# An explicit order of 3,392 tasks in place of a list scheduler, in a kernel of attention with memory and a gated feed-forward

## The chip, the cores and the metric

One core of a Trainium2 chip. The metric is the device time of one execution in microseconds (us), as the median of several runs.

## The reference, cut to what matters

`x` has 2,048 rows of 448. The result mixes two branches with a gate for each row:

```python
g = _sigmoid((x * gate_w).sum(-1, keepdims=True))
a = _A_ref(x, A_wq, A_wk, A_wv, A_wo, A_beta)   # 16 heads of 28, 4 segments of 512 rows
b = _B_ref(x, B_w1, B_w2)                       # silu(x @ w1) @ w2, 1792 wide
return g * a + (1 - g) * b
```

Branch A, for each segment s and head: softmax of the scores with a mask inside the segment, times the values; a memory read `phi(q) @ M / (phi(q) @ z)`, where M and z gather `phi(k)^T v` and `phi(k)` of the segments before; the two are mixed by a sigmoid of beta, and `wo` follows.

## The kernel before, in words

**How the work is tiled.** The core keeps 128 partitions. Each float32 operand of a product is split into two float16 halves, a high one and a low one, after a power of two found on the chip has scaled it; a product is then three float16 matmuls (high times high, low times high, high times low) that accumulate in one PSUM bank. `halves` makes the high half (L702 on ScalarE, or L704 on VectorE where both are allowed) and the low half through `rest` (L691 on VectorE as one instruction, or L693 and L694 on GpSimd as two). `product` (L728) issues the matmuls of one such product, cut into tasks of two to five matmuls.

**How it is staged.** First, in `project()`: the inputs are loaded, `scales` finds the powers of two (sums of squares, one small matmul with a matrix of ones at L564, four small VectorE instructions from L568 on), q, k and v are projected for the four segments (`proj`, `vproj`), and the memory is built and read (`memory`, `remember`, `retrieve`). The four value blocks of segment 0 are computed early in float32, before any scale is known (`vearly`, L1091, 16 tasks of two matmul records each). Then, for each of 16 groups of four heads, `maxima` finds the row maxima of the scores (L832 on TensorE, L840 and L845 on VectorE) and `attention` computes the scores again (L1468), their exponentials (L1473, ScalarE), the mask (L1476 and L1479, GpSimd), the halves (L1485 on ScalarE, L1489 on GpSimd) and the product with the values (L1502). The feed-forward runs beside it in two passes over blocks of 128 hidden columns (`unit`: L728 up, L1351 to L1356 with `evict` at L423 on ScalarE or L425 on VectorE, L1373 down). The second pass also applies `wo` to each block of 128 rows (`last_part`, L728 into a bank `sc`), adds it (L1585, L1589) and writes the output. The last row block of all cuts its down products at column 336, so that most of its result can be written before the rest.

**What sets the order.** The code above does not issue instructions; it calls `sch.add` once for each piece of work, with its engine (or a choice of two), a planned length, its inputs, the buffers it takes and a priority. There are 3,392 such tasks, numbered here from 0 in the order in which they are added. `Sched.run` then plays a list scheduler: of the tasks whose inputs are done it picks on each engine the one with the earliest planned start and the best priority, with a table `SHIFTS` of corrections to single priorities, and for a task that may run on two engines `start_of` compares the planned ends with a `SLACK`. What is picked is emitted at once. So each engine's queue is a fixed list in the program, worked off in that order; the semaphores make an instruction wait for its inputs, and everything behind it on its engine then waits too. The planned lengths are in `pe`, `act`, `dve`, `pool`, `few`, `scaled` and the like; at run time they play no part.

**The tasks that are spoken of below**

| tasks | what they are |
|---|---|
| 5, and 6 to 11 | matmuls of zeros: 8 in task 5 (L912), then six tasks of one (L917) |
| 54 to 69 | the early float32 products, four for each of the four row blocks (L1091) |
| 84, 74, 105, 94 | the small matmuls of `scales` for wv, for x of segment 0, for wk, for wq (L564) |
| 75, 85, 95, 106 | the VectorE instructions that follow 74, 84, 94, 105 (L568 to L572) |
| 40, 41 | the load of one quarter of wq, and its sum of squares on ScalarE (L545) |
| 96, 98, 100, 102 | the high halves of wq (96 VectorE, the others ScalarE); 97, 99, 101, 103 the low ones (L691) |
| 77, 79, 81, 83 | the low halves of x of segment 0 (L691); 91 one of wv |
| 124, 165, 166, 167 | first parts of the q products of groups 0 and 1 (L728); the parts after the first need the low halves of wq |
| 233, 234 | squares of the sizes of x of segment 1 (VectorE, L562) and their small matmul (L564); 443, 444 the same for segment 2 |
| 143 | the low half of phi(k) of group 0 (VectorE, L1080), which waits for a ScalarE instruction (L1078) |
| 217, 276 | the low half of q of group 3 (VectorE, L1033), and a k product of segment 1 (L728) that takes the PSUM bank which 217 reads |
| 239, 243, 445 | low halves of x of segment 1 (L691), and the instructions L568 to L572 of segment 2 |
| 968, 971 | low halves of two blocks of w1 |
| 2436, 2444, 2460 | evictions of the first three feed-forward blocks |
| 1006 | the first score matmul of the attention (L1468) |
| 3371 | the last task of the final row block's down product that is 336 columns wide (three matmuls, L1373) |
| 3383 to 3386, 3372 to 3375 | the final row block's `wo` product (11 matmuls), and its down product over the last 112 columns |

Of the kernel before, what the change touches and what calls it, by code (L numbers as in the profile page):

```python
# [50 lines left out]
SLACK = -0.26  # L51
# [5 lines left out]
FULL = 0.111  # L57
# [23 lines left out]
def VP(o, k):  # L81
# [3 lines left out]
PRICE = 191.19  # L85
PRICE2 = 269.85
SLACK2 = -0.48
# [18 lines left out]
SHIFTS = (  # L106
# [45 lines left out]
)  # L152


class Ring:
    def __init__(self, n, make, shared=True):
        self.n, self.make, self.seq, self.shared = n, make, [], shared

    def prev(self):
        k = len(self.seq) - self.n  # L160
# [1503 lines left out]
```

## Time and profile before

| what | us |
|---|---|
| median of three runs | 549.45 |
| lowest and highest of the three | 546.99, 551.03 |
| the profiled execution: its own time | 548.6 |
| the profiled execution: span from first to last instruction | 546.9 |
| TensorE busy, of the span | 536.6 |
| VectorE, ScalarE, GpSimd busy | 436.5, 392.4, 356.8 |

TensorE is busy for 98% of the span, VectorE for 80%, ScalarE for 72%, GpSimd for 65%. A busy TensorE is read with care, since the ends of matmuls are modelled in the trace: consecutive starts in the timeline tell its pace better than the busy time of a row. A view by windows gives, for each stretch of the span, the busy time and the number of instructions of each engine and the granted TensorE clock (`PEclk`, 1.00 is full speed). In a timeline each line is a run of like instructions with its start and its length, and in brackets the idle time of the engine before it and what ended that.

### The profile page before, as it was taken

Reading aid. Unit: us, or ns where it says so; the run is one execution under the profiler, and the core shown is the slowest. Engines: PE = TensorE matmul, PEld = TensorE weight load, DVE = VectorE, ACT = ScalarE, POOL = GpSimd, SP = SyncE. Lnnn points to the kernel's source line nnn. Section 1 sums busy time; section 2 is a strip of 40 time slices with the busy share of each in tenths; the row PEclk is TensorE's granted clock in tenths of the full one; section 3 lists DMA queues with packets and bytes.
Section 4 is the critical chain, followed back from the end, with each engine's and each line's share of the span. In section 5 each row is a group of like instructions: output and inputs, shape, how many; then the busy total and the mean of one; then the engine's idle time right before and its main releaser. Section 6 shows DMA issues by size and latency. Waiting matters only on the chain.

```text
span 546.9 us, 11691 instructions
## 1 busy us (share of the span) xinstructions
PE 536.6 (98%) x4083; PEld 295.3 (54%) x4083; DVE 436.5 (80%) x1065; ACT 392.4 (72%) x660; POOL 356.8 (65%) x542
## 2 busy tenths in 40 slices
PE   9899999999999999999999999999999999999997
PEld 3344555555544456555565555555555555455554
DVE  4889999999879977899765999779998258955553
ACT  5978987866546888888887988879987887501310
POOL 2128997354515778998898988898889997202220
PEclk9899999999999999999999999999999999999999
DMA  8678766535676333422323325555103211769973
GB/s 292 229 220 260 226 183 189 174 97 164 191 200 180 97 111 102 123 86 71 102 75 116 87 72 140 124 151 144 50 20 91 86 50 38 254 155 283 254 201 86
DMA packets 78059, 78.94 MB, mean 144 GB/s; under 512 B 44168, under 2 KB 67720, under 8 KB 78000
## 3 DMA queue, kind: packets, MB, share of 16 engines
q1 hardware_dynamic: 77424, 77.21, 49.1%
q10 hardware_dynamic: 576, 0.99, 0.6%
q8 instruction: 32, 0.52, 0.4%
q14 instruction: 27, 0.22, 0.1%
HBM read 48.41 MB, written 26.09 MB: 136 GB/s over the span
## 4 chain that ended last, share of the span: by engine, by line
PE 83%; DVE 9%; DMA 3%; POOL 2%; issue 1%; ACT 1%; SPq 0%; DVEq 0%; POOLq 0%; ACTq 0%
PE mm L728 22%; PE mm L1373 17%; PE sc L728 10%; PE cc L1373 6%; PE sc L1468 6%; PE cc L1502 6%; PE sc L832 5%; PE cc L728 4%; DVE sc L845 2%; PE sc L1091 2%; DMA rawf<-in_w_dram 1%; PE cc L1145 1%; PE cc L1221 1%; DVE ghl L1356 1%; DVE mm L1353 1%
## 5 line engine op out<-in xcount | busy, mean ns | idle before, releaser
L1489 POOL TENSOR_TENSOR phl<-pf,phl 128x384 f16<-128x384 f32 (+1 forms) x192 | 190.8, 1013 | 27.9 <-ACT phl L1485 27.3
L1473 ACT ACTIVATE pf<-sc,lift,es 128x512 f32<-128x512 f32 (+1 forms) x192 | 126.3, 702 | 26.2 <-PE sc L1468 22.1
L845 DVE CUSTOM_DVE_ANT_0 sc<-sc,mk 128x384 f32<-128x384 f32 (+2 forms) x192 | 105.1, 569 | 22.5 <-PE sc L832 20.7
L1373 PE MATMUL mm<-wb,ghl 128*128 128x448 f16 (+2 forms) x516 | 111.5, 348 | 0.0
L728 PE MATMUL mm<-xh,wa 128*128 128x512 f16 x429 | 108.7, 378 | 0.1
L1373 PEld LDWEIGHTS <-ghl 128*128 128x128 f16 x684 | 64.4, 97 | 53.7 <-issue 0.9
L1485 ACT ACTIVATE phl<-pf 128x1280 f16<-128x1280 f32 x64 | 80.8, 1265 | 9.8 <-POOL pf L1479 9.5
L728 PEld LDWEIGHTS <-wa 128*128 128x128 f16 x572 | 53.7, 97 | 53.4 <-issue 1.5
L1468 PE MATMUL sc<-ring 86*128 86x128 f16 (+3 forms) x256 | 59.9, 299 | 0.5 <-ACT pf L1473 0.3
L832 PE MATMUL sc<-ring 84*128 84x384 f16 (+3 forms) x256 | 57.9, 299 | 1.2 <-DVE mx L840 0.4
L739 POOL TENSOR_TENSOR ol<-ol,ml 128x448 f32<-128x448 f32 x12 | 14.0, 1170 | 53.7 <-DMA ol<-o_scr 36.2
L1502 PEld LDWEIGHTS <-phl 128*128 128x128 f16 x1280 | 41.9, 96 | 9.7
L728 PE MATMUL mm<-xh,wqs 128*128 128x512 f16 x176 | 43.7, 387 | 1.8 <-DVE wqs L704 1.8
L728 PE MATMUL mm<-xh,wks 128*128 128x512 f16 x176 | 43.6, 381 | 0.9 <-DVE stg L1033 0.9
L1479 POOL TENSOR_SCALAR_AFFINE_SELECT pf<-pf 128x384 f32<-128x384 f32 x64 | 33.7, 527 | 15.5 <-ACT pf L1473 15.0
L1502 PE MATMUL cc<-vg,phl 128*128 128x29 f16 (+1 forms) x1280 | 43.6, 182 | 0.0
L745 ACT ACTIVATE oh<-ol,os 128x448 f16<-128x448 f32 x16 | 10.7, 666 | 41.9 <-POOL ol L739 41.2
L1373 PE MATMUL cc<-wb,ghl 128*128 128x448 f16 x168 | 38.3, 352 | 0.0
L1351 ACT ACTIVATE th<-mm,ths 128x512 f32<-128x512 f32 x39 | 26.6, 682 | 15.2 <-PE mm L728 15.2
L728 PE MATMUL cc<-xh,wa 128*128 128x512 f16 x143 | 36.6, 378 | 0.0
L1468 PEld LDWEIGHTS <-ring 86*128 86x128 f16 x256 | 24.2, 97 | 23.0 <-issue 1.1
L728 PE MATMUL sc<-wos,oT 128*128 128x448 f16 x176 | 35.4, 352 | 0.0
(204 smaller groups left out, 923.0 us busy)
## 6 DMA issues: line engine op xcount, KB each, us to landing
rawf<-in_w_dram SPq DMA_DIRECT2D x26, 256.0 KB
rawf<-in_w_dram SPq DMA_DIRECT2D x28, 224.0 KB
v_scr<-vt SPq DMA_DIRECT2D x16, 232.0 KB
vg<-v_scr SPq DMA_DIRECT2D x16, 232.0 KB
xraw<-in_x_dram SPq DMA_DIRECT2D x14, 256.0 KB
q_scr<-stg SPq DMA_DIRECT2D x16, 224.0 KB
ring<-q_scr SPq DMA_DIRECT2D x16, 224.0 KB
k_scr<-stg SPq DMA_DIRECT2D x16, 224.0 KB
```

The lines of the kernel that those rows point to most:

```text
L728: nc.tensor.matmul(ps(), *p[i], start=(i == 0), stop=(i == n - 1))
L739: d = pool(530, lambda: nc.gpsimd.tensor_add(b.v, b.v, m.v), d, e, uses=[b, m], **k)
L832: nc.tensor.matmul(ps.v[:, u:u + n], rg.v[:KS, 0, hh, i * 128:(i + 1) * 128], rg.v[:KS, 1, hh, :n], start=i + t > 0, stop=(i + t > 0 or j ...
L845: nc.vector.tensor_tensor_reduce(r, r, MK[:, L - n:], 1.0, NEG, OP.add, OP.max, mx.v[:, hh, i:i + 1])
L1351: e1 = sact(L, lambda ps=ps, th=th: nc.scalar.activation(th.v, ps.v, AF.Tanh, scale=ths[:, s:s + 1]), m, takes=[th], uses=[ps], prio=p0)
L1373: nc.tensor.matmul(ps.v[:, lo:hi], g.v[:, y, sl], w.v[:, z, lo:hi], start=(j == 0 and i == 0), stop=(j == len(fs) - 1 and i == 2))
L1468: nc.tensor.matmul(ps.v[:, e:e + w], rg.v[:KK, 1, hh, j * 128:(j + 1) * 128], rg.v[:KK, 0, hh, j * 128:], start=True, stop=True)
L1473: ex.append(sact(e + 104, lambda b=b, ps=ps, pf=pf, e=e: nc.scalar.activation(pf.v[:, b, :e], ps.v[:, :e], AF.Exp, bias=lift, scale=es[:, ...
L1479: mk.append(pool(204, lambda pf=pf: nc.gpsimd.affine_select(pf.v[:, :, :128], pf.v[:, :, :128], [[0, 3], [1, 128]], OP.is_ge, 0.0, base=0, ...
L1485: hi = copy(1280, lambda hl=hl, flat=flat: nc.scalar.activation(hl.v[:, 0], flat(), AF.Copy), *mk, takes=[hl], uses=[pf], prio=p0 + 2)
L1489: low = pool(w - u + 22, lambda hl=hl, flat=flat, u=u, w=w: nc.gpsimd.tensor_sub(hl.v[:, 1, u:w], flat()[:, u:w], hl.v[:, 0, u:w]), low, u ...
L1502: nc.tensor.matmul(p[:, i, :2 - z], hl.v[:, z, u:u + 128], vg.v[:, j, hh, :2 - z], start=(z == zs[0] and i == 0), stop=(z == zs[-1] and j ...
```

## The change

The list scheduler is taken out: `offer`, `matmuls`, the candidate lists, the prices and slacks, and the table `SHIFTS`. In their place stands a table `ORDER` that names every one of the 3,392 tasks once, in the order in which it is to be emitted. A negative entry -1-i means task i on the second of its two engines (ScalarE or VectorE: VectorE; VectorE or GpSimd: GpSimd). Seven planned lengths are edited. Against the order that the list scheduler gives, all engines keep their tasks but for 42 that change between two engines: 9 from VectorE to GpSimd (six low halves, 87, 449, 968, 971, 3015 and 3109, and three sums), 1 from GpSimd to VectorE, 19 from VectorE to ScalarE, 13 from ScalarE to VectorE. Within the engines, 465 of TensorE's 1,201 tasks, 206 of ScalarE's and 270 of VectorE's lie outside the longest run of tasks that both orders have in common; TensorE's move by 2.6 places in the mean and by 27 at most.

```diff
-SHIFTS = (
-    (14, 17, 239.16), (41, 41, 29.48), (64, 64, 83.58), (65, 65, -15.52), (95, 95, 613.1), (97, 101, -24633.04),
...
+ORDER = (
+    3, 22, 5, 6, 7, 8, 9, 10, 34, 30, 0, 13, 14, 32, 26, 18, 36, 15, 17, 28, 11, 20, 54, 55, 19, 16, 24, 23, 27, 29, 25, 73,
+    35, 44, 31, 33, 38, 46, 37, 50, 56, 57, 84, 66, 85, 1, 2, 48, 74, 75, 67, -81, 116, 4, 45, 12, 52, 39, -83, 81, 90, 68,
+    42, 40, 47, 58, 78, 847, 91, 163, 59, 79, 69, 70, 51, 49, 53, 43, 41, 83, 187, 122, 21, 60, 61, 156, 76, 105, 94, 106,
+    95, 111, 100, 77, -97, 101, 98, 99, 62, 211, 63, 113, 97, 102, 117, 848, 103, 157, 158, 64, 65, 849, 153, 124, 114, 165,
+    166, 414, 167, 107, 108, 109, 334, 112, 86, 125, 71, 110, 850, 123, 144, 159, 88, 126, 146, 148, 127, 851, 261, 152, 168,
...
+    961, 959, 963, 1006, 2435, 972, 966, 1067, 1066, 2443, 2454, 2455, 2436, 2456, 2457, 1010, 1008, 2444, 2437, 1068, 2450,
+    1005, 973, 967, 2445, 1007, 2462, 1069, 2458, 1011, 2451, 1009, 1020, 974, -2453, 969, 2453, 1156, -969, 2459, 1070,
...
+    3283, 3353, 3333, 3362, 3357, 3363, 3364, 3334, 3335, 3382, 3370, 3379, 3383, 3384, 3385, 3386, 3371, 3372, 3373, 3374,
+    3375, 3330, 3365, 3331, 3366, 3367, 3348, 3387, 3388, 3349, 3389, 3390, 3391,
 )
...
-        while wait is None or wait:
-            best = None
-            for eng, c in self.cand.items():
...
+        while wait if wait is not None else self.at < len(ORDER):
+            i = ORDER[self.at]
+            self.at += 1
+            t = self.tasks[max(i, -1 - i)]
+            t.eng = list(t.costs)[i < 0]
+            s = self.start_of(t, t.eng)
+            assert t.nd == 0 and s is not None, "order"
...
-        return sch.add(("DVE", "POOL"), (0.135 + 0.00104 * cols, 0.3 + 0.0051 * cols), lambda e: fn(eng[e]), deps, port=True, **k)
+        return sch.add(("DVE", "POOL"), (0.135 + 0.00104 * cols, 0.3 + 0.0054 * cols), lambda e: fn(eng[e]), deps, port=True, **k)
...
-                ready = [dve(75, lambda: nc.vector.tensor_mul(v, v, v), *ready, prio=prio)]
+                ready = [dve(250, lambda: nc.vector.tensor_mul(v, v, v), *ready, prio=prio)]
...
-        VREADY[s] = few(1, gate, SCALED[NSEG - 1 - s], SCALED[WV], prio=prio)
+        VREADY[s] = few(0, gate, SCALED[NSEG - 1 - s], SCALED[WV], prio=prio)
...
-        EREADY[s] = few(10, scores, PREADY[s], SCALED[WQ], SCALED[WK], prio=prio + 0.5)
+        EREADY[s] = few(8, scores, PREADY[s], SCALED[WQ], SCALED[WK], prio=prio + 0.5)
```

The three other length edits have the same form (`kscale` 2 to 4, `qscale` 2 to 0.5, `derive` 6 to 7.4).

More of the change, by code (lines that the diff above doesn't have):

```diff
@@ L50 @@
 WIRE = 4.3
-SLACK = -0.26
 LOP = 210.09
@@ L82, in VP @@
     return o + VA + VS * k if o or k > VF else -1.0 + 0.1 * k
-PRICE = 191.19
-PRICE2 = 269.85
-SLACK2 = -0.48
 PVRUNS = [((1, 0), 1)]
@@ L217, in __init__ @@
         self.free = {e: 1.0 for e in self.HOP}
-        self.cand = {e: [] for e in self.HOP}
         self.count = 0
@@ L222, in __init__ @@
         self.wire, self.lands = WIRE, []
-        self.price, self.slack = PRICE, SLACK
-        self.shift = {i: d for a, b, d in SHIFTS for i in range(a, b + 1)}
+        self.tasks, self.at = [], 0
     def add(self, eng, dur, fn, deps=(), takes=(), uses=(), prio=0.0, lat=0.0, port=False, load=None):
         self.count += 1
-        prio += self.shift.get(self.count, 0.0)
         t = Task(eng, dur, fn, [d for d in deps if d is not None], list(takes), list(uses), (prio, self.count), lat, port)
@@ L236, in add @@
                 t.nd += 1
-        if t.nd == 0:
-            self.offer(t)
-        return t
-    def offer(self, t):
-        for e in t.costs:
-            self.cand[e].append(t)
+        self.tasks.append(t)
+        return t
     def ready(self, t, eng):
@@ L265, in start_of @@
                 s = max(s, b.last.end + self.HOP[b.last.eng])
-        if len(t.costs) > 1:
-            o = [e for e in t.costs if e != eng][0]
-            if self.locked(t, eng, s) + t.costs[eng] > self.locked(t, o, max(self.free[o], s)) + t.costs[o] + self.slack:
-                return None
         return self.locked(t, eng, s)
@@ L280, in uncovered @@
         return max(0.0, t.lead - self.tail) if s < self.free["PE"] + 1e-6 else 0.0
-    def matmuls(self, ready):
-        leads = sorted(t.lead for t in ready)
-        def rank(t):
-            nxt = leads[0] if t.lead != leads[0] or len(leads) == 1 else leads[1]
-            if len(leads) == 1 or t.lead == leads[0] and leads[1] != leads[0]:
-                nxt = FULL
-            return t.prio[0] + self.price * (max(0.0, t.lead - self.tail) + max(0.0, nxt - t.tail)), t.prio[1]
-        return min(ready, key=rank)
     def run(self, until=None):
         wait = set(until) if until is not None else None
-        while wait is None or wait:
-            best = None
-            for eng, c in self.cand.items():
-                first = pick = None
-                can = []
-                for t in c:
-                    s = self.start_of(t, eng)
-                    if s is None:
-                        continue
-                    can.append((s, t))
-                    if first is None or s < first - 1e-9 or (s <= first + 1e-9 and t.prio < pick.prio):
-                        first, pick = s, t
-                if eng == "PE" and pick is not None and first < self.free["PE"] + 1e-9:
-                    pick = self.matmuls([t for s, t in can if s <= first + 1e-9])
-                if pick is not None and (best is None or first < best[0]):
-                    best = (first, pick, eng)
-            if best is None:
-                assert wait is None and not any(self.cand.values()), "stuck"
-                return
-            s, t, t.eng = best
-            for e in t.costs:
-                self.cand[e].remove(t)
+        while wait if wait is not None else self.at < len(ORDER):
[5 more added lines that the diff above has]
+            assert t.nd == 0 and s is not None, "order"
             if t.eng == "PE":
@@ L345, in run @@
                 n.nd -= 1
-                if n.nd == 0:
-                    self.offer(n)
             if wait is not None:
@@ L638, in kscale @@
         if s < NSEG - 1:
-            KREADY[s] = few(2, go, SCALED[NSEG - 1 - s], SCALED[WK], *deps, prio=prio)
+            KREADY[s] = few(4, go, SCALED[NSEG - 1 - s], SCALED[WK], *deps, prio=prio)
     def qscale(s, prio):
@@ L646, in go @@
             by(z, z, UP, op0=OP.min)
-        PQREADY[s] = few(2, go, SCALED[NSEG - 1 - s], SCALED[WQ], prio=prio)
+        PQREADY[s] = few(0.5, go, SCALED[NSEG - 1 - s], SCALED[WQ], prio=prio)
     def others(s, prio, bds, own, t_own, t_gh):
@@ L685, in go @@
             by(hso[:, s:s + 1], wide[:, s:s + 1], hs[:, s:s + 1])
-        return few(6, go, SCALED[W1], EREADY[s], GDONE[s], prio=prio)
+        return few(7.4, go, SCALED[W1], EREADY[s], GDONE[s], prio=prio)
     def rest(e, out, a, s, b):
@@ L1320, in infini_mix @@
     BK["cc"].give(BK["mm"])
-    sch.price, sch.slack = PRICE2, SLACK2
     fes = ExitStack()
```

196 rows, old and new, of tables (ORDER, SHIFTS) are left out of this document.

## The prediction

> **What bounds the kernel now.** I read the page first, then its stages by windows, then TensorE's waits and timeline in the stages where it is not full. The page:
>
> ```profile
> span 546.9 us, 11691 instructions
> PE 536.6 (98%) x4083; PEld 295.3 (54%) x4083; DVE 436.5 (80%) x1065; ACT 392.4 (72%) x660; POOL 356.8 (65%) x542
> ```
>
> The windows (per engine: busy us, instructions; then the granted clock):
>
> ```profile
> 0.00:25.00 25.00, 22.14 (x61) 9.38 (x62) 15.77 (x54) 18.07 (x44) 5.86 (x32) 0.94 0.82 278
> 25.00:75.00 50.00, 48.07 (x292) 25.93 (x291) 47.45 (x101) 43.88 (x103) 33.66 (x57) 0.99 0.74 224
> 75.00:160.00 85.00, 84.96 (x548) 47.37 (x547) 77.79 (x173) 57.26 (x120) 45.16 (x87) 1.00 0.56 166
> 160.00:200.00 40.00, 38.53 (x276) 19.98 (x274) 36.77 (x99) 30.81 (x48) 23.04 (x30) 1.00 0.52 143
> 200.00:540.00 340.00, 339.84 (x2890) 190.91 (x2889) 256.46 (x638) 242.42 (x347) 249.05 (x337) 1.00 0.43 118
> 540.00:546.90 6.90, 3.02 (x26) 1.76 (x24) 2.26 (x5) 0.00 (x0) 0.00 (x0) 1.00 0.29 100
> ```
>
> TensorE sets the time everywhere. From 75 to 160 and from 200 to 540 us it is idle for 0.04 + 0.16 us, and a new order can win nothing there. Its idle time is 2.86 us at the start, 1.93 between 25 and 75, 1.47 between 160 and 200, and 3.88 at the end. Every task stays, so TensorE's work stays; an order is worth what it takes from these four numbers, and from the clock.
>
> **The change, part by part.** The code that schedules emits nothing, and the mended lengths emit nothing either: order and engine now come from the table, and the planned start is used in an assertion alone. Their cost is nil and needs no cover. What is left are the places of the tasks, one stage after the other.
>
> *Start.* TensorE's timeline, VectorE's beside it, then two windows:
>
> ```profile
> 4.43 1.37 PE L917 MATMUL mm<-maskb 128*128 128x512 bf16 x4
> 5.63 3.40 PE L1091 MATMUL sc<-raw,xraw 128*128 128x450 f32 x8
> 18.82 1.02 PE L1091 MATMUL sc<-raw,xraw 64*128 64x450 f32 x2
> 19.77 0.60 PE L917 MATMUL mm<-maskb 128*128 128x512 bf16 x2
> 20.21 0.28 PE L564 MATMUL cc<-sums,ones 128*128 128x5 f32 x2
> 22.32 2.74 PE L728 MATMUL mm<-xh,wqs 128*128 128x512 f16 x6 [1.82 <-DVE wqs L704]
> 25.87 3.62 PE L728 MATMUL mm<-xh,wqs 128*128 128x512 f16 x16
> 29.33 4.26 PE L728 MATMUL mm<-xh,wks 128*128 128x512 f16 x19
> ```
> ```profile
> 15.65 0.61 ACT L545 ACTIVATE junk<-raw 128x512 bf16<-128x512 f32 x1
> ```
> ```profile
> 20.54 0.16 DVE L568 TENSOR_REDUCE few<-cc 128x1 f32<-128x5 f32 x1 [0.87 <-PE cc L564]
> 22.84 2.73 DVE L691 SCALAR_TENSOR_TENSOR wqs<-raw,up,wqs 128x512 f16<-128x512 f32 x4
> ```
> ```profile
> 22.30:25.60 3.30, 3.28 (x8) 1.20 (x9) 3.30 (x6) 3.30 (x8) 0.00 (x0) 0.50 0.29 107
> 25.60:27.00 1.40, 1.40 (x8) 0.64 (x7) 1.40 (x3) 1.40 (x4) 0.27 (x1) 1.00 0.36 47
> ```
>
> The last square of wq (task 41) starts on ScalarE at 15.65 and is done before 16.5, but its matmul (94) stands behind all early products and two matmuls of zeros and runs at 20.21. So the scale of wq is late, TensorE idles 1.82 us, and then the clock is granted at 0.50: 8 matmuls in 3.30 us. At full speed 16 take 29.33 - 25.87 = 3.46, so 8 take 1.73, and the slow stretch loses 1.6. Together 3.4 us.
>
> In the table the two matmuls of zeros come before the early products, and 94 before the last four of these (62 to 65). An early product takes 3.40 / 4 = 0.85 us, so 94 runs with 3.4 us of work left behind it. It is not late itself: load 40 and square 41 keep their places on their queues. Ahead of VectorE's part of it (95) stand more pieces than before, and it ends, by my adding up of VectorE's rows, at about 19.2, with the high halves of wq by about 20.7. The early products, behind zeros that now run 0.4 us longer at the front, end between 20.5 and 21.1 (74 now comes after five of them in place of eight and may wait half a microsecond for x's sums). So 124 starts near 21.0, at full clock. Of the gain of 1.3 + 1.6 a part goes at once: the four low halves of wq take 2.73 us on VectorE and end near 23.4, and TensorE, now faster than they, waits some 0.6 us for them. I take 2.3 us. The bounds are 0 (the chain ends where it did) and 3.4 (both losses go).
>
> The Trainium skill (TensorE: Matmul & The Clock Gate, "What's actually happening") says that the clock is halved after an idle window of about 3.4 us, and that these windows run freely. The slow stretch has that length (3.30 us and a rest), but the gap ahead of it was 1.82 us, so here the trace differs: a window that was only half idle was enough. By free windows some executions of before would not have the slow stretch, this step would be worth 0.7 us in them, and the sum would be 2.8.
>
> *25 to 75 us.* TensorE's waits, and VectorE's rows beside the two longest:
>
> ```profile
> PE mm L728 <- DVE stg L1033: 0.9, 1, 0.9
> PE cc L564 <- DVE sums L562: 0.7, 2, 0.4
> ```
> ```profile
> 39.39 0.68 DVE L1080 SCALAR_TENSOR_TENSOR phk<-sc,spk,phk 128x448 f16<-128x448 f32 x1 [1.75 <-ACT phk L1078]
> 39.99 0.15 DVE L562 TENSOR_TENSOR sums<-sums 128x5 f32<-128x5 f32 x1
> 45.95 1.05 DVE L562 TENSOR_TENSOR sums<-sums 128x5 f32<-128x5 f32 x1
> 50.30 1.29 DVE L1033 SCALAR_TENSOR_TENSOR stg<-mm,stg 128x512 f16<-128x512 f32 x2
> ```
> ```profile
> 45.82 1.15 POOL L694 TENSOR_TENSOR xh<-xraw,xh 128x512 f16<-128x512 f32 x1
> ```
>
> Here the queue's head blocks. Task 143 (L1080) waits 1.75 us for ScalarE, with 233 (L562) behind it, for whose matmul TensorE waits. In the table 233 stands five tasks ahead of 143. The 0.9 us are 276's, for the bank that 217 (L1033) reads; 217 goes up nine places, ahead of 239, 445 and 243. These two waits go. The second L562 took 1.05 us in place of 0.15: it ends with GpSimd's L694, at 47.0. It can meet such a piece again. I take 1.3 of the 1.6 us; bounds 0.5 and 1.9.
>
> The Trainium skill (SBUF — State Buffer, on the shared port pair) says that VectorE with two SBUF inputs and a reading GpSimd exclude each other for a whole instruction. The row of 1.05 us agrees. It speaks against the nine pieces moved to GpSimd; what that could cost is the last rival but one.
>
> *160 to 200 us*, waits of TensorE, and the mean durations (third number from the bar) of what moves:
>
> ```profile
> PE sc L832 <- DVE mx L840: 0.4, 1, 0.4
> PE sc L1468 <- ACT pf L1473: 0.3, 1, 0.3
> PE sc L832 <- DVE mx L845: 0.2, 1, 0.2
> ```
> ```profile
> L425 DVE TENSOR_SCALAR ghl<-mm 128x512 f16<-128x512 f32 x23 | 15.8, 686 | 0.5
> L691 DVE SCALAR_TENSOR_TENSOR wa<-rawf,up,wa 128x512 f16<-128x512 f32 x13 | 10.5, 824 | 0.9 <-ACT wa L702 0.9
> L693 POOL TENSOR_SCALAR xraw<-xraw,up 128x512 f32<-128x512 f32 x6 | 9.4, 1572 | 1.0 <-ACT xh L702 1.0
> L694 POOL TENSOR_TENSOR xh<-xraw,xh 128x512 f16<-128x512 f32 x6 | 7.1, 1184 | 0.5
> ```
>
> VectorE is the late one, busy for 36.77 of 40 us. The table takes from it just ahead of this stage 968 and 971 (0.82 us each, to GpSimd, busy 23.04) and evictions 2436, 2444 and 2460 (0.69 each, to ScalarE, busy 30.81): 3.7 us. And the first score matmul (1006) comes five tasks earlier. I take 1.0 of the 1.47 us; bounds 0 and 1.47.
>
> *End.*
>
> ```profile
> 538.48 1.87 PE L1373 MATMUL mm<-wb,ghl 128*128 128x336 f16 x12
> 540.19 2.25 PE L728 MATMUL sc<-wos,oT 128*128 128x448 f16 x11
> 542.47 0.68 DVE L1585 SCALAR_TENSOR_TENSOR ya<-sc,gas,pl 128x448 f32<-128x448 f32 x1 [1.67 <-PE sc L728]
> 543.24 0.81 DVE L1589 SCALAR_TENSOR_TENSOR y<-mm,ogs,ya 128x336 f32<-128x336 f32 x2
> ```
>
> The `wo` product is followed by L1585 and L1589, which set the end. Twelve matmuls of 336 columns take 540.19 - 538.48 = 1.71 us; the table puts three of them (3371) behind that product, under L1585. The product ends 0.43 us earlier, and so does the kernel. Bounds 0 and 0.43.
>
> *Elsewhere* 465 of TensorE's 1,201 tasks stand otherwise in stretches that are full, so they can only lose. If a tenth of 340 us ran like 160 to 200 us, that is 34 x 1.47 / 40 = 1.2. I take half, 0.6; bounds 0 and 3.
>
> Sum: 2.3 + 1.3 + 1.0 + 0.4 - 0.6 = 4.4 us. The profiled execution took 548.6 us, span and 1.7 around it, so it would take 544.2. It lay 0.85 under the median shown, 549.45; on that, I forecast 545.0, 0.8% less. About 1%, or 5.5 us, is what a measurement of this kernel can tell from no change.
>
> **Rivals.**
>
> *All waits go* and nothing new comes: 3.4 + 1.6 + 1.47 + 0.43 + 0.2 elsewhere = 7.1, so 542.3. For it speaks that each wait above has a task that moved; against it that the low halves of wq still follow one another on VectorE.
>
> *The start stays late.* 95 stands behind more VectorE pieces than 94's new place suggests (81, 91, 79, 83, 106). If 106 and 95 end after 20 us, the gap and the slow clock stay, and only 2.1 us are won: 547.3.
>
> *GpSimd's pieces hold VectorE back; slower.* 968 and 971 on GpSimd take 1.57 + 1.18 = 2.75 us each, 5.5 together, where VectorE took 1.65. If VectorE waits them out, as L562 did at 45.95, or the first feed-forward products that need these halves do, TensorE is short of 5.5 us of work just where scores begin. A gap beyond 1.82 us also brings the slow clock, 1.6 more. It decides from about 4.4 us of such idle time; in full it is 7.1 lost against 4.4 won: 552.2. Against it: GpSimd is idle for 17 of 40 us there.
>
> *The order doesn't matter:* semaphores already leave TensorE little idle time and new waits of the same size replace the old: 549.5.
>
> **How the numbers follow.** The forecast 0.54 (its terms give 543 to 547), all waits go 0.18, the start stays late 0.16, GpSimd slower 0.06, no change 0.06. Faster by over 1% is below 543.95: most of the second case and a third of the first, 0.34. Slower by over 1% (above 554.9) is the worse half of the slower rival, 0.03; the rest, 0.63, is within 1%. The range from 541.5 to 549.0 leaves out the two last cases and little at the low end.
>
> **What would show it.** Right: L564 for wq near 17.7 us with L1091 behind it, the first L728 by 21.3 us, the clock at 1.00 after it, no wait of L564 on L562 near 39 us, L728 not waiting for L1033 near 50, TensorE idle under 0.7 us from 160 to 200, and L1373 at 336 columns behind the last L728. Wrong: a granted clock of 0.50 after the first microseconds, new waits of TensorE between 200 and 540 us, or a span above 546.

## The result, and the profile after

| | before | after |
|---|---|---|
| median, us | 549.31 (4 runs, 546.99 to 551.03) | 541.91 (4 runs, 541.10 to 542.12) |
| profiled execution: own time, span | 548.6, 546.9 | 541.86, 539.7 |

The ratio is 0.9865, with a 95% interval from 0.9827 to 0.9903: the table makes the kernel 1.35% faster, 7.4 us (5.3 to 9.5). The forecast was 545.0 in a range from 541.5 to 549.0.

First the head of the page after:

```profile
span 539.7 us, 11686 instructions
PE 533.7 (99%) x4083; PEld 295.1 (55%) x4083; DVE 429.9 (80%) x1051; ACT 396.0 (73%) x666; POOL 376.3 (70%) x556
```

Then the windows that were shown of before (per engine: busy us and instructions; granted clock ahead of the two DMA columns):

```profile
0.00:25.00 25.00, 23.80 (x71) 9.89 (x72) 16.45 (x55) 17.48 (x45) 6.85 (x31) 1.00 0.71 250
25.00:75.00 50.00, 49.47 (x304) 27.02 (x303) 48.47 (x104) 45.21 (x108) 38.57 (x57) 1.00 0.77 231
75.00:160.00 85.00, 84.41 (x549) 47.38 (x548) 78.30 (x174) 59.97 (x123) 46.98 (x94) 1.00 0.63 185
160.00:200.00 40.00, 39.96 (x306) 21.78 (x305) 36.12 (x102) 33.25 (x51) 31.69 (x40) 1.00 0.42 120
```

TensorE is idle for 0.53 us between 25 and 75 us where it was 1.93, and for 0.04 between 160 and 200 where it was 1.47; the clock is 1.00 in all four rows. One idle stretch is new, 0.59 us between 75 and 160. The list of TensorE's waits after has three rows left beside one at the start that both kernels have (a line's number is 72 higher than before, further down 71: L904 was L832, L1147 was L1075, L1422 was L1351):

```profile
PE sc L904 <- ACT th L1422: 0.6, 1, 0.6
PE sc L1147 <- DVE ph L1130: 0.5, 1, 0.5
PE sc L1163 <- DMA raw<-in_wv_dram: 0.2, 1, 0.2
```

TensorE's timeline at the start:

```profile
17.53 0.61 PE L636 MATMUL cc<-sums,ones 128*128 128x5 f32 x4
18.00 3.46 PE L1163 MATMUL sc<-raw,xraw 128*128 128x450 f32 x8
21.39 5.01 PE L800 MATMUL mm<-xh,wqs 128*128 128x512 f16 x22
26.25 4.05 PE L800 MATMUL mm<-xh,wks 128*128 128x512 f16 x18
```

The small matmuls for wk and wq (105 and 94) are one row at 17.53, four early products follow them, and the first scaled product begins at 21.39 with no gap in front of it and no slow stretch behind it: 22 matmuls in 26.25 - 21.39 = 4.86 us, 0.22 each.

**Where the 7.2 us of the span come from.** Idle time alone doesn't say, so the two timelines are compared at instants at which TensorE has done exactly the same set of tasks in both kernels; there the difference of the two starts is what the new order is ahead. Rows of before, then of after, each the first behind such an instant:

```profile
81.99 1.46 PE L728 MATMUL mm<-xh,wqs 128*128 128x512 f16 x6
...
162.38 1.46 PE L728 MATMUL cc<-xh,wa 128*128 128x512 f16 x6
...
188.00 0.73 PE L1373 MATMUL mm<-wb,ghl 128*128 128x448 f16 x3
...
394.12 0.38 PE L832 MATMUL sc<-ring 84*128 84x512 f16 x1 [0.16 <-DVE mx L845]
```
```profile
58.08 0.73 PE L800 MATMUL sc<-wvs,xh 128*128 128x450 f16 x3
...
77.35 1.46 PE L800 MATMUL mm<-xh,wqs 128*128 128x512 f16 x6
...
158.45 0.38 PE L904 MATMUL sc<-ring 84*128 84x128 f16 x4 [0.57 <-ACT th L1422]
...
181.44 0.38 PE L1539 MATMUL sc<-ring 86*128 86x512 f16 x1
...
387.12 0.38 PE L904 MATMUL sc<-ring 84*128 84x512 f16 x1
```

| same work done at (before) | at (after) | ahead | gained since the line above |
|---|---|---|---|
| 29.33 | 26.89 | 2.4 | 2.4 |
| 63.45 | 58.08 | 5.4 | 2.9 |
| 81.99 | 77.35 | 4.6 | -0.7 |
| 162.38 | 158.45 | 3.9 | -0.7 |
| 188.00 | 181.44 | 6.6 | 2.6 |
| 394.12 | 387.12 | 7.0 | 0.4 |
| span's end, 546.9 | 539.7 | 7.2 | 0.2 |

(26.89 lies inside the row at 26.25, three matmuls of 0.215 us on; 63.45 in a row of seven of before that starts at 62.80.) Three stretches won, two lost 0.7 us each to new waits, and the 340 us in which TensorE was full won 0.4.

The loss at 61 us, in the timeline after, VectorE's, GpSimd's and TensorE's rows:

```profile
60.11 1.65 DVE L1130 SCALAR_TENSOR_TENSOR ph<-pe,pp 112x512 f32<-112x512 f32 x1
...
60.05 1.16 POOL L766 TENSOR_TENSOR xh<-xraw,xh 128x512 f16<-128x512 f32 x1
...
61.91 0.57 PE L1147 MATMUL sc<-ident,ph 112*128 112x112 f32 x4 [0.53 <-DVE ph L1130]
```

VectorE's instruction took 1.65 us; it starts 0.06 us behind a GpSimd piece that ends at 61.21, and TensorE waits for it. (Without that piece beside it the same instruction takes 0.67 us, in experiment 11 and also in 7, whose order is that of after up to there: so this wait comes in some executions of the order and not in others.) And the end, TensorE's rows, then VectorE's:

```profile
532.77 2.25 PE L800 MATMUL sc<-wos,oT 128*128 128x448 f16 x11
534.85 1.18 PE L1444 MATMUL mm<-wb,ghl 128*128 128x336 f16 x15
...
535.05 0.68 DVE L1656 SCALAR_TENSOR_TENSOR ya<-sc,gas,pl 128x448 f32<-128x448 f32 x1 [0.99 <-PE sc L800]
536.07 0.81 DVE L1660 SCALAR_TENSOR_TENSOR y<-mm,ogs,ya 128x336 f32<-128x336 f32 x2 [0.33 <-PE mm L1444]
```

The three wide matmuls (3371) now run behind the `wo` product, in the row of 15. L1656 starts 7.42 us earlier than its counterpart at 542.47; L1660, which then waits 0.33 us for those three matmuls, only 7.17 earlier than at 543.24.

### The profile page after: what moved, and what is told of

Read it like the earlier page. It is cut to its first block, busy times and chain, and to the rows that moved or that the text cites. A ratio compares the mean times of both kernels' runs of the same rounds, so it can differ in the third digit from the quotient of the medians.

```text
span 539.7 us, 11686 instructions
## 1 busy us (share of the span) xinstructions
PE 533.7 (99%) x4083; PEld 295.1 (55%) x4083; DVE 429.9 (80%) x1051; ACT 396.0 (73%) x666; POOL 376.3 (70%) x556
## 4 chain that ended last, share of the span: by engine, by line
PE 94%; DMA 2%; ACT 1%; DVE 1%; issue 0%; SPq 0%; DVEq 0%; ACTq 0%
PE mm L800 30%; PE mm L1444 17%; PE sc L800 10%; PE cc L1444 7%; PE sc L1539 6%; PE sc L904 6%; PE cc L1573 6%; PE cc L800 5%; PE sc L1163 1%; DMA raw<-in_wv_dram 1%; PE cc L1217 1%; PE cc L1293 1%; PE sc L1147 1%; DMA xraw<-in_x_dram 1%; PE mm L1163 1%
## 5 line engine op out<-in xcount | busy, mean ns | idle before, releaser
L1560 POOL TENSOR_TENSOR phl<-pf,phl 128x384 f16<-128x384 f32 (+1 forms) x192 | 190.9, 1015 | 17.1 <-ACT phl L1556 15.9
L1544 ACT ACTIVATE pf<-sc,lift,es 128x512 f32<-128x512 f32 (+1 forms) x192 | 128.3, 705 | 24.0 <-PE sc L1539 21.3
L917 DVE CUSTOM_DVE_ANT_0 sc<-sc,mk 128x256 f32<-128x256 f32 (+2 forms) x192 | 106.0, 568 | 27.0 <-PE sc L904 24.4
L800 PE MATMUL mm<-xh,wa 128*128 128x512 f16 x440 | 111.4, 378 | 0.0
L1444 PE MATMUL mm<-wb,ghl 128*128 128x448 f16 (+2 forms) x486 | 107.2, 347 | 0.0
L1556 ACT ACTIVATE phl<-pf 128x1280 f16<-128x1280 f32 x64 | 80.8, 1266 | 5.7 <-POOL pf L1547 3.1
L1539 PE MATMUL sc<-ring 86*128 86x128 f16 (+3 forms) x256 | 61.0, 299 | 0.0
L904 PE MATMUL sc<-ring 84*128 84x256 f16 (+3 forms) x256 | 60.3, 299 | 0.6 <-ACT th L1422 0.6
L1444 PE MATMUL cc<-wb,ghl 128*128 128x448 f16 x198 | 44.9, 352 | 0.0
L1581 DVE TENSOR_REDUCE oraw<-cc 128x116 f32<-128x232 f32 x64 | 25.1, 393 | 19.7 <-PE cc L1573 19.5
L1550 POOL TENSOR_SCALAR_AFFINE_SELECT pf<-pf 128x384 f32<-128x384 f32 x64 | 34.2, 534 | 7.8 <-ACT pf L1544 6.4
L1422 ACT ACTIVATE th<-mm,ths 128x512 f32<-128x512 f32 x40 | 27.4, 684 | 15.9 <-PE mm L800 13.2
```

The source lines that it names most:

```text
L800: nc.tensor.matmul(ps(), *p[i], start=(i == 0), stop=(i == n - 1))
L904: nc.tensor.matmul(ps.v[:, u:u + n], rg.v[:KS, 0, hh, i * 128:(i + 1) * 128], rg.v[:KS, 1, hh, :n], start=i + t > 0, stop=(i + t > 0 or j ...
L917: nc.vector.tensor_tensor_reduce(r, r, MK[:, L - n:], 1.0, NEG, OP.add, OP.max, mx.v[:, hh, i:i + 1])
L1422: e1 = sact(L, lambda ps=ps, th=th: nc.scalar.activation(th.v, ps.v, AF.Tanh, scale=ths[:, s:s + 1]), m, takes=[th], uses=[ps], prio=p0)
L1444: nc.tensor.matmul(ps.v[:, lo:hi], g.v[:, y, sl], w.v[:, z, lo:hi], start=(j == 0 and i == 0), stop=(j == len(fs) - 1 and i == 2))
L1539: nc.tensor.matmul(ps.v[:, e:e + w], rg.v[:KK, 1, hh, j * 128:(j + 1) * 128], rg.v[:KK, 0, hh, j * 128:], start=True, stop=True)
```

## The experiments

The theory: the semaphores' waits go where the prediction placed them, each by its own move, and the table changes nothing else. The rivals: the table or the lengths do something by themselves; what is won early is given back later; single moves would do as much; engines rather than places matter. All kernels are the code after with another table (4 changes one call besides), so their line numbers are those of after, or one higher in 7 and, from the changed call on, in 4. "Control" is experiment 1, and "ahead of control" compares the profiled executions at equal work, as above. Ratios are to the kernel before, run on the same chip. In the diffs of 1, 2, 5 and 6 the table after stands on the minus side; in 3, 4, 9 and 10 the order of before does.

**1. The old order as a table.**

```diff
 ORDER = (
-    3, 22, 5, 6, 7, 8, 9, 10, 34, 30, 0, 13, 14, 32,
+    30, 3, 0, 22, 12, 18, 5, 32, 34, 36, 17, 24, 16, 1,
...
```

> The list order of before, written out as a table, under the code of after with its mended lengths. If table and lengths emit nothing by themselves, this is the program of before: 549.3 us, ratio 1.000, and a clock of 0.50 for 3.4 us near 22 us in every execution, so a mean clock of 0.997. If the windows of the clock run freely, some executions have no slow stretch (mean clock 0.999 or 1.000) and are some 1.6 us shorter. If the mended lengths matter by themselves, the time lies below 549.

Measured: 548.69 (10 runs) against 548.68 (31 runs), ratio 1.0001 [0.9983, 1.0019]. In both traces TensorE, VectorE, ScalarE and GpSimd run the same instructions in the same order. Table and lengths cost and bring nothing that can be measured. Its profiled execution brought a second finding: span 546.0, clock 1.00 throughout, with the same gap as before:

```profile
22.05 1.78 PE L800 MATMUL mm<-xh,wqs 128*128 128x512 f16 x6 [1.82 <-DVE wqs L776]
```

So the same program with the same 1.82 us of idle time has the slow stretch in one execution and not in another. How often, the mean granted clock of an execution tells: in the profiled execution of before, with its one slow stretch, it is 0.997. It is 0.997 or less in 8 of control's 10 executions and in 57 of the 69 of before that stand beside these experiments, and 0.999 or 1.000 in the rest. The 57 took 549.0 us in the mean, the 12 others 548.7.

Against control's profiled execution the table is ahead by 0.9 us at the start rather than 2.4, by 2.6 at the 77 us instant, and by 6.1 us at the end of TensorE's work. The first six steps of the table above are 0.9, 2.3, -0.5, -0.5, 2.4 and 0.7 against it. So between two executions of one program a step differs by up to 0.65 us, beside the 1.5 of the clock.

**2. Only the start: after's table to about 28 us, then the old order.**

```diff
-    928, 236, 198, 143, 375, 178, 415, 182,
+    928, 236, 198, 118, 115, 104, 155, 160, 177, 178, 143, 958, 182,
...
```

> The table of after up to the first 14 parts of q and k products (all engines, some 28 us), then the order of before. Places theory: the start wins 2.4 us, as the progress of TensorE in the two traces has it, and no more: 546.9 us. Rival, that the start only looks shorter because later work is put off: the gain is given back by 75 us, and the time is 549.

Measured: 547.67 (10 runs), ratio 0.9978 [0.9963, 0.9993]. At equal work it is 1.8 us ahead of control at 37 us and 0.7 behind at 50. The waits of TensorE that took it:

```profile
PE mm L800 <- DVE stg L1105: 1.9, 1, 1.9
PE cc L1217 <- DVE phk L1152: 1.2, 2, 0.8
```

The first is the wait for 217 that was 0.9 us in before. TensorE came earlier, VectorE's queue did not, and the wait took up the difference: the start alone is mostly given back 20 us later. It is worth 0.2%.

**3. One move: 94 ahead of the last two early products (64, 65), of 105 between them and of the zeros, in the old order.**

```diff
-    847, 64, 82, 849, 261, 105, 144, 65, 334, 83, 145, 148, 10, 149, 11, 106, 156, 374, 94, 152,
+    847, 82, 849, 261, 144, 334, 83, 145, 148, 149, 156, 94, 64, 105, 65, 10, 11, 106, 374, 152,
```

> The order of before with one task moved: 94, the small matmul for the scale of wq, ahead of the last two early products and the two matmuls of zeros. Places theory: its VectorE part (95) starts when 106 ends, near 19.6 us in place of 20.5, the first L800 comes near 21.5 in place of 22.3, the gap shrinks to 1.0 us and the clock stays at 1.00: about 2 us won, 547.3. If the whole rearrangement of VectorE is needed, the first L800 stays at 22.3 and nothing is won, 549.3.

Measured: 548.70 (10 runs), ratio 0.9999 [0.9981, 1.0018]. TensorE's row, then VectorE's that explains it:

```profile
21.99 0.49 PE L800 MATMUL mm<-xh,wqs 128*128 128x512 f16 x1 [1.43 <-ACT wks L774]
...
20.85 0.69 DVE L1187 SCALAR_TENSOR_TENSOR vt<-mm,rvf,vt 128x448 f16<-128x448 f32 x1 [0.38 <-ACT gate L1185]
21.45 0.48 DVE L776 TENSOR_SCALAR wqs<-raw,up 128x512 f16<-128x512 f32 x1
```

94 is early, but on VectorE, whose order this edit leaves as it was, task 158 (L1187) stands ahead of the high half of wq (96, L776) and waits for ScalarE. The gap is 1.43 us in place of 1.82, and the slow stretch is there too. Moving the one late task isn't enough; the queues behind it have to be rearranged with it.

**4. The gap filled: the zeros behind 94, the second of them nine matmuls.**

```diff
-    148, 10, 149, 11, 106, 156, 374, 94, 152,
+    148, 149, 106, 156, 374, 94, 10, 11, 152,
...
-            END1.append(pe(half(L), lambda: nc.tensor.matmul(
-                wb.v, maskb, maskb[:, None, :].to_broadcast([128, 4, 128]), start=True, stop=True),
+            many = 9 if _ == MORE - 1 else 1
+            END1.append(pe(half(L), lambda many=many: [nc.tensor.matmul(
+                wb.v, maskb, maskb[:, None, :].to_broadcast([128, 4, 128]), start=True, stop=True) for _ in range(many)],
```

> The order of before, with 94 ahead of the two matmuls of zeros and the second of these made nine, so that 2.2 us of zeros fill the gap ahead of the first L800; one part alone, the clock. Clock theory: no slow stretch, and the 1.6 us that it lost are won, with 0.3 us more for 94: 547.4. Rival, that the slow stretch ran under the low halves of wq (VectorE until 25.6 us): TensorE only waits where it was slow, and less than 0.7 us is won: 548.6.

Measured: 548.09 (10 runs), ratio 0.998 [0.9965, 0.9995].

```profile
19.75 2.32 PE L990 MATMUL mm<-maskb 128*128 128x512 bf16 x10
21.90 0.67 PE L800 MATMUL mm<-xh,wqs 128*128 128x512 f16 x2
```

No gap and no slow stretch, at the price of ten matmuls of zeros: the mean granted clock is 0.999 or 1.000 in all ten executions, where 27 of the 31 of before have 0.997 or less. What remains is 0.6 us in the median (0.3 to 1.9 by the interval). That is the size that the rival named, less than the 1.5 by which control stands ahead of before just behind the stretch. Its reason isn't borne out: control, at full clock, is 1.6 us ahead of before at 28 us and still 1.8 at 480. But at the end of TensorE's work 0.9 are left. How much of the 1.5 lasts to the end of an execution stays open; this only bounds the clock's part of the whole gain.

**5. After's table to about 75 us, then the old order.**

```diff
-    434, 371, 482, 483, 484, 875, 387,
+    434, 371, 875, 876, 454, 297, 457, 458, 305,
...
```

> The table of after for the first 120 TensorE tasks and all that goes with them (some 75 us), then the order of before. Against a control execution at full clock, after is 0.9 us ahead by 30 us and 2.6 ahead by 75. Places theory: that lead is kept, since the rest has the waits of before and no more: 548.7 - 2.6 = 546.1. Rival, seen where only the start was changed: queues filled for one order and emptied by another bring new waits at the seam, and the lead is gone: 548.5.

Measured: 549.41 (10 runs) against 549.10 (15), ratio 1.0015 [0.9996, 1.0034]. At equal work it is 3.9 us ahead of control at 50 us, and still so behind 70; at 89.4 us 0.4 are left, and by 180 it is 1.5 behind. The wait, and the windows around it:

```profile
PE cc L1217 <- DVE amr L1299: 3.2, 1, 3.2
```
```profile
85.87:89.28 3.41, 0.35 (x2) 0.10 (x1) 0.64 (x2) 1.28 (x3) 2.60 (x11) 1.00 0.44 150
89.28:92.69 3.41, 3.25 (x20) 2.45 (x20) 3.41 (x10) 2.30 (x7) 2.08 (x3) 0.50 0.44 135
```

At the seam TensorE finds an instruction of the old order whose VectorE work has not come, waits 3.2 us, and gets the half clock for it. This kernel can't tell what the first 75 us are worth, only that it isn't kept by an order that was made for another arrival.

**6. After's table to about 190 us, then the old order.**

```diff
-    1140, 1135, 2517, 1143, 2541, 1064, 1339, 1124, 1002,
+    1140, 1135, 2517, 1339, 1278, 1064, 1002, 1124, 2551,
...
```

> The same to some 190 us, past the stage where scores begin. Places theory: the lead is 4.6 us there, and after that TensorE has nothing left to win but some 0.3 us and the end: 544.1. If the moves between 200 and 540 us are worth more than the traces show, it stays above 545.

Measured: 541.47 (4 runs), ratio 0.9875 [0.9838, 0.9911], the same as the whole table within the intervals. As far as these (some 2 us to either side) can tell, all of the gain is made in the first 190 us, and the new order of the other 350, the end included, is worth nothing.

**7. After, with 968, 971, 2436, 2444 and 2460 back on VectorE.**

```diff
-    2443, 2454, 2455, 2436, 2456, 2457, 1010, 1008, 2444, 2437,
+    2443, 2454, 2455, -2437, 2456, 2457, 1010, 1008, -2445, 2437,
...
-    2453, 1156, -969, 2459,
+    2453, 1156, 968, 2459,
...
```

> The table of after, with five tasks put back on VectorE: the low halves 968 and 971 and the evictions 2436, 2444, 2460. If VectorE's relief by 3.7 us is what won the 2.3 us from 160 to 200 (prediction), TensorE waits for VectorE there again and the time is 543 to 544. If the order alone did it (scores earlier, score and feed-forward tasks dealt out otherwise), it stays at 541.9.

Measured: 542.80 (6 runs), ratio 0.9901 [0.987, 0.9931]; the median is 0.9 us above after's. At equal work it is 1.5 us ahead of the profiled execution of after at 60 us, 0.9 at 158 and 0.7 behind at 169: 2.2 us go there. Part of that is a wait for a transfer at 157.6, where after waits 0.6 for ScalarE:

```profile
PE sc L905 <- DMA ring<-k_scr: 1.2, 1, 1.2
```

The five engines matter by a microsecond or so, in the direction that the prediction had; the intervals of 7 and of after overlap, so this is likely and not shown. Of the lead at 60 us, 0.7 is the wait at 61, which this execution doesn't have, though nothing was changed up to there: VectorE's instruction started 0.6 us ahead of the GpSimd piece, and took its plain length.

```profile
58.82 0.67 DVE L1131 SCALAR_TENSOR_TENSOR ph<-pe,pp 112x512 f32<-112x512 f32 x1
```

**8. After, with two moves against the two new waits:** 287 (the transposes that wait for L1130) three places back, behind 389, and 1069 (the score matmul that waits at 158) behind 2463. As the edit was made, 1069 also came to stand behind 1071, another score matmul.

```diff
-    345, 300, 287, 900, 877, 257, 389, 390,
+    345, 300, 900, 877, 257, 389, 287, 390,
...
-    2462, 1069, 2458, 1011,
+    2462, 2458, 1011,
...
-    2459, 1070, 1021, 2463, 1071, 1072,
+    2459, 1021, 2463, 1071, 1069, 1070, 1072,
```

> The table of after with two TensorE tasks moved behind one ready product each: 287 (the transposes that wait 0.7 us for VectorE near 61 us) behind 389, and 1069 (the first scores of the second group, which wait 0.7 us near 157) behind 2463. If these waits are TensorE's own to avoid, 1.3 us are won: 540.6. Rival: the later tasks hold up their banks and the wait comes back further on: 541.9.

Measured: 543.64 (4 runs), ratio 0.9907 [0.987, 0.9944]: 1.7 us above after in the median. The wait at 61 is gone, but:

```profile
162.54 0.32 PE L904 MATMUL sc<-ring 84*128 84x384 f16 x1 [1.64 <-DVE mx L917]
```

**9. The two moves of the prediction's second step alone:** in the old order, 233 ahead of 143, and 217 ahead of 239.

```diff
-    177, 212, 178, 143, 958, 182, 233, 928,
+    177, 212, 178, 958, 182, 233, 143, 928,
...
-    239, 933, 480, 263, 223, 205, 228, 290, 553, 445, 864, 264, 243, 291, 866, 244, 867, 217, 446,
+    933, 480, 263, 223, 228, 290, 864, 866, 244, 217, 239, 205, 553, 445, 264, 243, 291, 867, 446,
```

> The order of before with two VectorE tasks moved: 233 ahead of 143, and 217 ahead of 239. Places theory, one part alone: the wait of L636 on L634 near 39 us (0.3 to 0.6) and that of L800 on L1105 near 50 (0.9) go, 1.3 us: 547.6 beside 548.9. Rival, as in the runs in which a part of the new order was set into the old: the tasks that they pass become late in their place, and the time is that of before.

Measured: 548.62 (10 runs) against 548.95 (23), ratio 0.9994 [0.998, 1.0008]. The wait near 39 us is gone and one remains:

```profile
PE mm L800 <- DVE stg L1105: 0.6, 1, 0.6
```

Against control it gains 2.0 us from 27 to 50 us and loses 1.3 of them again by 62. Two moves don't make the 1.3 us that I ascribed to them.

**10. The old order with after's engines for the five tasks.**

```diff
-    2446, 969, 2442, -2437, 2437, 959,
+    2446, 969, 2442, 2436, 2437, 959,
...
-    2462, 968, 2458, 1006, 971, 1008,
+    2462, -969, 2458, 1006, -972, 1008,
...
```

> The order of before, with the engines of after for 968, 971, 2436, 2444 and 2460 and nothing else: the complement of the run that put them back. There they were worth 0.9 us. If VectorE's relief works in any order, 0.9 us are won here: 548.0. If it is only of use where the scores start early, 548.9.

Measured: 549.49 (10 runs), ratio 1.0015 [0.9996, 1.0034]. TensorE is busy for 37.27 of the 40 us from 160 to 200, less than before's 38.53, with new waits:

```profile
PE cc L1573 <- POOL phl L1560: 1.1, 1, 1.1
PE sc L904 <- DMA ring<-k_scr: 1.1, 2, 0.7
```

GpSimd's two longer pieces (968, 971) run until 166.76. Its masks for the first exponentials (L1550, L1547) stand behind them, at 166.71 in place of control's 163.25; ScalarE's L1556 waits 1.59 us for these, and GpSimd's L1560, for which the product with the values waits, comes after that. So what relieves VectorE brings waits of its own in the old order; the time is not measurably longer by them.

**11 and 12. The two moves apart.** 11 has only 287 behind 389; 12 has that and 1069 behind 2463, but ahead of 1071.

```diff
-    345, 300, 287, 900, 877, 257, 389, 390,
+    345, 300, 900, 877, 257, 389, 287, 390,
```
```diff
-    2459, 1021, 2463, 1071, 1069, 1070, 1072,
+    2459, 1021, 2463, 1069, 1070, 1071, 1072,
```

> The table of after with 287 alone moved behind 389. The run that moved two tasks lost 2.1 us near 160 us and won 0.5 near 61. Places theory: 0.5 won and nothing lost: 541.4. Rival: no order is better than another by less than what changes from one execution to the next: 541.9.

> The same, and 1069 moved behind 2463 but, other than in the earlier run, still ahead of 1071, so that TensorE fills these two banks in the order in which VectorE's queue empties them. If it was the exchange with 1071 that cost 2.1 us there, the wait of 0.7 us near 157 goes and nothing comes: 540.8. If it was 1069's being later, the loss comes again: 543.5.

Measured: 541.51 (6 runs, 541.06 to 544.17), ratio 0.9882 [0.9856, 0.9907], and 541.80 (5 runs), ratio 0.9876 [0.9854, 0.9898]. In 11 the wait at 61 us is gone, with VectorE's row at the plain length:

```profile
59.50 0.67 DVE L1130 SCALAR_TENSOR_TENSOR ph<-pe,pp 112x512 f32<-112x512 f32 x1
```

Its span, 539.0, is 0.7 us under that of after, as the price of the wait has it, but its median is not apart from after's by more than the executions differ, and since 7 lacks the wait without the move, the move is not shown to be what took it away. Two of the six executions, 543.86 and 544.17, have a mean granted clock of 0.997; the other four, at 1.000, took 541.06 to 541.87. So the new order is not safe from the slow clock either; where it struck is in no trace here.

12 missed its 540.8: the wait near 157 was not won, and at equal work it loses 0.9 us to after between 157 and 165 (8 loses 2.2). Between 8 and 12 only the order of 1069 and 1071 differs. At equal work 12 goes from 0.6 us ahead of 8 at 158 us to 2.2 ahead near 162 and 1.8 from 165 on. VectorE takes the maxima of 1069 (its task 1070) first in both, so in 8, where TensorE runs 1071 first, a bank stays taken for longer. That this is the whole reason is argued and not shown; that the exchange costs some 1.2 us at that place is what the two traces show, while the intervals of the two times overlap. No version is measurably better than the table.

## Why the prediction was right, and where it was too small

The direction and the mechanism were right: the waits named went, at the tasks named, and nothing between 200 and 540 us was hurt. The forecast was 3.1 us too high, at the median: the time lies 0.4 us above the low end of the range, and a gain of over 1% had been given 0.34, less than the 0.63 for a change within 1%. By its own terms, gained in the profiled pair:

| step | predicted | measured |
|---|---|---|
| start | 2.3 | 2.4 |
| 25 to 75 us | 1.3 | 2.2 (2.9 won, 0.7 lost at 61) |
| 160 to 200 us | 1.0 | 1.9 (2.6 won, 0.7 lost at 158) |
| elsewhere | -0.6 | 0.4 |
| end | 0.4 | 0.2 |
| sum (of the unrounded) | 4.4 | 7.2 |

**Start.** The right size by luck, from two errors that cancel. The first product came at 21.39 where I had 21.0, so the gap gave 0.9 and not 1.3; the clock gave 1.5 of 1.6; and the 0.6 that I took off for the low halves of wq was not lost: the 22 matmuls from 21.39 on run at 0.22 us. Experiments 1 to 4 add what one profiled pair could not show: the 1.5 of the clock are in that execution of before and, by the mean granted clock, in some five of six, but not in all, so that against control's execution, at full clock, the start gave 0.9. The prediction had 0.7 for that case, by the windows that run freely by the Trainium skill (TensorE: Matmul & The Clock Gate, "What's actually happening"), and the trace agrees. And neither moving 94 alone (ratio 0.9999) nor the start alone (0.9978) wins what the table does.

**25 to 75 and 160 to 200: the terms that were mis-sized.** I took them from TensorE's idle time, 1.93 and 1.47 us, as the most that could be won. It is not the most. Rows of before's timeline, around one listed wait and another that is hardly listed:

```profile
178.30 0.33 PE L832 MATMUL sc<-ring 84*128 84x384 f16 x1
178.46 0.60 PE L728 MATMUL cc<-xh,wa 128*128 128x512 f16 x2
178.90 0.38 PE L1468 MATMUL sc<-ring 86*128 86x512 f16 x1
179.50 0.32 PE L832 MATMUL sc<-ring 84*128 84x384 f16 x1 [0.23 <-DVE mx L845]
...
185.33 0.32 PE L832 MATMUL sc<-ring 84*128 84x384 f16 x1 [0.21 <-ACT pf L1473]
185.70 0.73 PE L1373 MATMUL mm<-wb,ghl 128*128 128x448 f16 x3
```

A lone matmul of 512 columns is drawn 0.38 us long, though in a run the next one starts 0.22 after it. From 178.90 to 179.50 are 0.60 us, so 0.38 are lost, where the trace lists 0.23 of idle time: each wait costs its idle time and 0.16 more. A short pause isn't listed at all: from 185.33 to 185.70 are 0.37 us for a matmul of 384 columns, where the same form at 178.30 takes 0.16, so 0.21 are lost, and no idle time stands at 185.70. Between the instants 162.38 and 188.00 before needed 25.62 us, after 181.44 - 158.45 = 22.99 for the same work: 2.63 us won, from a stretch with 1.47 listed. The same holds for 25 to 75 us (2.9 won of 1.93; against control 2.3 of its 1.57) and for the new waits (0.53 and 0.57 listed, 0.7 lost each). Of the reason given for 160 to 200 us, VectorE's relief, experiment 7 takes back 0.9 us in the median, which is not clear of the differences between executions; the larger part of the 2.6 is then the order's, but no run parts the two. (In the prediction's rows of 160 to 200 us the mean duration is the second number from the bar, not the third.)

**Elsewhere.** I expected a tenth of the full stretch to get waits and got none; by the same rule the two listed waits of before were worth more than their 0.2. By experiment 6 the moves there neither win nor lose anything that can be measured.

**End.** The product came 0.43 us earlier as forecast, but L1660 waited for the three matmuls put behind it; 0.2 were left. The step overlooked that these matmuls feed the last instruction too.

**The rivals.** *All waits go* named 542.3, nearest to what came, but not by its own sum: it counted 7.1 of idle time, while in fact more was lost before and two new waits took 1.4 back. *GpSimd's pieces hold VectorE back* happened in its mechanism, at 61 us rather than at the scores, for 0.7 us instead of 7.1, and not in every execution; the Trainium skill (SBUF — State Buffer, "Who interferes with whom") has that rule, and the rows agree for one kind of GpSimd piece: 1.65 us beside L766, which reads two inputs. Beside L765, which reads one input from SBUF and ran from 58.47 to 60.04 in experiment 11, the same VectorE instruction took its plain 0.67. In the old order the moved pieces do make a wait (experiment 10). *The start stays late* and *the order doesn't matter* are out by the start's rows and by the ratio. What none of the cases had: the steps don't add. Each alone (2, 3, 9, 10) is worth some 0.2% at most in the ratio; a TensorE that is earlier waits at the next place where its partner's queue is not.

What stays open: how much of the gain each step has by itself in an order that is otherwise the new one. Experiments 2 and 5 were to tell, and their seams, with waits up to 3.2 us, hide it. Nor does a run show how much of the clock's 1.5 us at the start lasts to the end of an execution: 4 gives 0.6 us (0.3 to 1.9) from a kernel that pays for its own cure, and the executions of before with a full clock are 0.3 us shorter in the mean than the others.

## What to carry to other kernels

Count what an engine that sets the time loses by the starts of its instructions at equal work, not by listed idle time: here each wait cost 0.16 us more than its row says, and short ones had no row. Where TensorE is 98% busy, expect to remove a wait only by moving its whole chain on all queues; here a single task or a single stage moved forward met the next queue that had not moved, and most of the gain was gone within some 20 us. Look at more than one execution before a wait is put down to the order: the one at 61 us was in some and not in others. Let an engine's relief be judged in the order in which it will run: the same five tasks on other engines brought new waits in one order and saved perhaps a microsecond in the other.

## What the runs showed of the hardware that was not expected

The slow clock comes in windows of 3.41 us, and all changes of the granted clock in one execution lie on one grid of that step, which is placed differently in each execution. (In before's trace the clock changes at 22.18, 25.60 and 547.84 us, and 522.24 us are 153 steps of 3.413; in after's it changes at 6.45 and 538.93, 156 steps apart.) Windows of that grid around the gap, of before, of the single move (3), of control, and of experiment 10:

```profile
18.77:22.18 3.41, 1.73 (x9) 0.82 (x7) 2.17 (x11) 2.30 (x5) 1.30 (x5) 1.00 0.76 262
22.18:25.60 3.42, 3.28 (x8) 1.20 (x9) 3.42 (x7) 3.42 (x8) 0.00 (x0) 0.50 0.31 114
```
```profile
18.73:22.14 3.41, 1.98 (x8) 0.69 (x6) 2.45 (x11) 2.08 (x5) 1.35 (x4) 1.00 0.41 136
```
```profile
17.78:21.19 3.41, 2.44 (x10) 1.17 (x8) 2.14 (x11) 2.61 (x7) 0.85 (x4) 1.00 0.77 276
21.19:24.60 3.41, 2.41 (x11) 0.98 (x11) 3.41 (x7) 3.41 (x7) 0.44 (x2) 1.00 0.50 173
```
```profile
20.75:24.17 3.42, 1.65 (x7) 0.70 (x8) 3.32 (x9) 3.42 (x6) 1.13 (x5) 1.00 0.62 223
```

In before the window from 18.77 has TensorE busy for 1.73 of 3.41 us, and the next one is at 0.50. In 3 it was busy for 1.98, in 9 for 1.58, and the next one was at 0.50 as well. In control a border cuts the same gap, TensorE is busy for 2.44 and 2.41 us in the two windows, and nothing follows. In 10 nearly the whole gap lies in one window, busy for 1.65, and nothing follows either. So a window that is half idle can put TensorE back by 1.5 us, and which executions of a program pay hangs at least in part on where the grid lies; the Trainium skill (TensorE: Matmul & The Clock Gate, "What's actually happening") says that the windows run freely, and the rows agree, but not that they have to be idle throughout. Idle time alone does not decide: the windows of before and 3 held small matmuls, zeros and a product of 64 rows, that of 10 full products. That the kind of work counts is a guess that no run here was made to test.
